# Two turns of activations by 32x32 blocks on VectorE, with feature rows numbered to match

## The chip, the cores and the metric

The kernel runs on one core of a Trainium2 chip. The metric is the device time of one execution in microseconds (us), the median of several runs. Every run gives one time; one further execution was recorded by the hardware profiler, and all rows quoted below come from that one.

## The reference, cut to what matters

One transformer block in float32 with S = 2048 tokens, D = 1024, 32 heads of 32, and an inner width of 3584:

```python
qkv = layernorm(x) @ wqkv                      # q, k, v by head
pq, pk = q @ w_phi, k @ w_phi                  # per head, 32x32
phi = concat(softmax(p), softmax(-p))          # for q and for k
o = phi_q (phi_k^T v) / (phi_q (phi_k^T 1) + 1e-6)
h = x + o @ wo
out = h + relu(layernorm(h) @ w1) @ w2
```

Both layer norms work on rows of tokens, and both products after them contract over the features. TensorE contracts over partitions, so x and h have to be turned: tokens on partitions before, features on partitions after.

## The kernel before

All large products run on TensorE with each float32 operand split in two float32r parts, a high and a low one, and three matmuls for each product (`mm3`, L180 to L183). A **step** is one `mm3`: three matmuls of 128x128 weights against 512 columns. The work of TensorE is a fixed list of **items**; an item has 8 steps before the MLP and 4 in it. Everything else is placed by hand: `when(step, f, ...)` puts the call of `f` behind the given step, and the engines then work their own rows in that order, each engine in order.

The items come in this sequence. Tokens are cut in 16 tiles of 128 (`t` = 0 to 15), in two halves of eight.

- Key and value items (`kv`) of the first half, four slabs of eight, then query items (`q`), two slabs of eight. Then the same for the second half. A slab uses the same 8 weight units for its eight tiles. Turned x stands in eight buffers `xT`, so that a tile of the second half is turned while the second query slab of the first half runs: tile `t` is normalised, turned by eight TensorE transposes (two bursts of four, `ln_turn`, L250), and copied out of PSUM as high part (ScalarE, L177) and low part (VectorE, L178).
- Attention's products (`at_num`, L678), spread over later items. Their inputs are turned by VectorE (`at_turn`, L664).
- 32 `wo` items, which give h. `wo_add` (L728) adds x on VectorE, `wo_store` (L731) writes h to DRAM. `ln_pair` then takes h back, two tiles at a time (one of each quarter of the tokens: the MLP's products are done by a scheme of seven products on sums of blocks, `UP` and `DOWN`), normalises them (L243), turns them by TensorE (L250 and L758, four bursts of four for a pair), copies them out of PSUM (L252, L759), forms the sums, and `ln_store` writes the seven operands `hs`. Four pairs belong to the first half (`b` = 0, during the `wo` items) and four to the second (`b` = 1, during the first half's up projection).
- Up projection and down projection of the MLP (`up_item`, `down_item`), first half, second half. `hT` is the turned h as the matmuls stream it.

Weights come through `Units`: SyncE's DMA queue loads a unit in one of 6 raw buffers, ScalarE copies the high part (L124), VectorE or GpSimd forms the low part (L128), into a ring of 10. In a slab 8 of the 10 are held, so the next slab's units 3 to 8 are split only as the last item of the old slab lets go of its units.

SyncE's queue (SP) issues nearly all DMAs, in order: weights, x, h, `hs` and the MLP's intermediate tensors. A DMA that waits for its data holds up all behind it.

Of the kernel before, what the change touches and what calls it, by code (L numbers as in the profile page):

```python
# [15 lines left out]
P = 128  # L16
# [123 lines left out]
def kernel(  # L140
# [68 lines left out]
    def ln_load(key, parts):  # L209
        xin[key] = xlp.tile([P, D], F32, name="xl") if key[0] == "x" and key[1] >= HT and key[1] % 4 > 1 else \  # L210
            lnp.tile([P, D], F32, name="xin")
        n = D // len(parts)
        for j, p in enumerate(parts):
            sp.dma_start(xin[key][:, j * n:(j + 1) * n], p)

    def ln_stats(key):
        src = xin[key]
        st = lnp.tile([P, 2, 6], F32, name="st", bufs=4)
# [21 lines left out]
    def ln_norm(key):  # L240
        sc, src = xst.pop(("s", key[1]) if key[0] == "x" and key[1] >= HT else key), xin.pop(key)
        xnt[key] = src if key[0] == "h" else fp_ln.tile([P, D], F32, name="xn")
        act.activation(xnt[key], src, AF.Identity, bias=sc[:, 1:2], scale=sc[:, 0:1])  # L243

    def ln_turn(key, j, dst=None):

        xn = xnt[key]
        pt = tp_bank().rearrange("p (k n) -> p k n", k=4)
        for k in range(4):
            pe.transpose(pt[:, k, :], xn[:, (4 * j + k) * P:(4 * j + k + 1) * P], ident)  # L250
        if dst is None:
            act.activation(xn[:, j * 512:(j + 1) * 512], pt.rearrange("p k n -> p (k n)"), AF.Copy)  # L252
            return
# [79 lines left out]
    def load(key, t):  # L333

        kind = key[0]
        if kind == "kv":
            _, hf, s, k = key
            sp.dma_start(t[:, 0:256], wpk[s][k])
            sp.dma_start(t[:, 256:512], wv[s, k])
        elif kind == "q":  # L340
            _, _, s, k = key
            sp.dma_start(t, wpq[s][k])
        elif kind == "wo":
            _, hf, c = key
            sp.dma_start(t, wo[hf, c])
        elif kind == "a":
            sp.dma_start(t, ad[key[1:]])
        else:
            _, _, m, p = key
            w = 1 if kind == "w1" else 2  # L350
            sp.dma_start(t, block(w, p, *{1: (0, 0), 2: (1, 0), 3: (1, 1)}[m]) if m < 4
                         else td[w, p][:, {5: 0, 7: 3 - w, 4: w, 6: 3}[m], :])

    def block(w, p, r, c):
# [359 lines left out]
    def wo_pair(tiles, hf, half, keys):  # L714
# [4 lines left out]
        for k in range(8):  # L719
# [5 lines left out]
            yield  # L725

    def wo_add(t, hf):
        v.tensor_add(xh[t, hf], wo_ps.pop((t, hf)), xh[t, hf])  # L728

    def wo_store(t, hf):  # L730
        sp.dma_start(hd[t][:, hf * 512:(hf + 1) * 512], xh.pop((t, hf)))  # L731

    def ln_pair(b, i, stage):

        keys = [("h", HT * b + 4 * r + i) for r in range(2)]
        if stage == 0:
            for key in keys:  # L740
                ln_load(key, [hd[key[1]]])
        elif stage == 1:
            for key in keys:
                ln_stats(key)
        elif stage == 2:
            for key in keys:
                ln_power(key)
        elif stage == 3:
            for key in keys:
                ln_norm(key)  # L750
        elif stage in (4, 5, 6):
            ln_turn(keys[stage // 6], stage != 4)
        elif stage == 7:
            x1, x2 = (xnt[key] for key in keys)
            s12 = (mp or hp).tile([P, 2, 512], F32, name="s12", bufs=1)
            pt = tp_bank()
            for k in range(4):
                pe.transpose(pt[:, k * P:(k + 1) * P], x2[:, k * P:(k + 1) * P], ident)  # L758
            act.activation(x2[:, 0:512], pt, AF.Copy)  # L759
            v.tensor_add(s12[:, 0, :], x2[:, 0:512], x2[:, 512:])  # L760
            v.tensor_sub(x2[:, 0:512], x1[:, 0:512], x2[:, 0:512])
            sums[b, i] = s12
        elif stage == 8:
            x1, s12 = xnt[keys[0]], sums[b, i]
# [12 lines left out]

    sums, hT = {}, {}

    def h_load(b, m, g):  # L780

        lo = hT[m][:, 1, :, 2 * g * P:2 * (g + 1) * P].rearrange("p k (i n) -> p k i n", i=2)
        for i in range(2):
            sp.dma_start(f32(lo[:, :, i, :]), hs[b, m][:, 2 * g + i, :].rearrange("p (k n) -> p k n", k=4))

    def h_parts(m, g):

        return (hT[m][:, s, :, 2 * g * P:2 * (g + 1) * P] for s in range(2))

# [167 lines left out]
    for t in range(1, NT):  # L957
# [4 lines left out]
        else:  # L962
# [12 lines left out]
        for j in range(2):  # L975
            when(stages[4 + j], ln_turn, ("x", t), j, lambda t=t: xT[t])
# [121 lines left out]
    LN2 = ((0, 9, 12, 17, 24, 25, 26, 27, 29, 36), (0, 18, 26, 32, 40, 42, 44, 46, 50, 60))  # L1100
# [219 lines left out]
```

## Time and profile before

| | |
|---|---|
| median of 3 runs | 1880.31 us (1879.95 to 1880.78) |
| the profiled execution's own time | 1881.49 us |
| its span, first to last instruction | 1879.7 us |
| granted TensorE clock | 1.000 |
| busy: TensorE matmul, weight load | 1872.6 us (100%), 1540.3 us |
| busy: VectorE, ScalarE, GpSimd | 1063.6, 741.0, 976.9 us |
| DMA | 433.21 MB, mean 230 GB/s |

PE is TensorE's matmuls, PEld its weight loads, DVE is VectorE, ACT ScalarE, POOL GpSimd, SPq the DMA queue of SyncE. A row of the timeline has the start in us, the time in us, the engine, the line, the operation, what it writes and reads, the shape and a count. Rows of grouped instructions end with busy time and the mean of one in ns, then idle time before them and what ended it. Matmuls overlap, and their ends are modelled: of PE, starts are to be read.

### The profile page before, as it was taken

The page shows a single profiled execution, that of the slowest core. Times are in us where ns is not written, and L with a number is a line of the kernel's source. Part 1 is how long each engine was busy: PE and PEld are TensorE (multiplying, and loading weights), DVE is VectorE, ACT ScalarE, POOL GpSimd, SP SyncE. Part 2 cuts the span into 40 slices and gives each one's busy share as a digit, 9 for nine tenths or more (in the row PEclk, how much of TensorE's full clock was granted, in tenths as well). Part 3 has the DMA queues.
Part 4 walks back from the last instruction along what each step waited for, and adds up shares of the span by engine and source line. Part 5 has one row for each costly group of instructions (what it writes and reads, how often), then busy time and mean ns, then how long its engine had stood idle before and what let it go on. Part 6 is the DMA issues. An engine that isn't in the chain of part 4 may idle for free.

```text
span 1879.7 us, 31869 instructions
## 1 busy us (share of the span) xinstructions
PE 1872.6 (100%) x11630; PEld 1540.3 (82%) x11630; DVE 1063.6 (57%) x1714; ACT 741.0 (39%) x1264; POOL 976.9 (52%) x956
## 2 busy tenths in 40 slices
PE   9999999999999999999999999999999999999999
PEld 7888888888888888888888888888888888888887
DVE  7788688677789777455444664444433333343333
ACT  5322244222233122355455554444444444444442
POOL 3778733677745988223343234445444444444443
PEclk9999999999999999999999999999999999999999
DMA  6889875454475567886877997877877677777775
GB/s 214 268 280 312 269 262 180 148 155 141 140 232 190 203 216 237 264 254 209 263 233 241 312 297 248 264 246 259 275 239 216 201 230 239 237 213 220 216 215 177
DMA packets 293036, 433.21 MB, mean 230 GB/s; under 512 B 24208, under 2 KB 150160, under 8 KB 292880
## 3 DMA queue, kind: packets, MB, share of 16 engines
q1 hardware_dynamic: 263712, 390.26, 65.3%
q10 hardware_dynamic: 29168, 40.93, 6.5%
q8 instruction: 91, 1.49, 0.3%
q14 instruction: 65, 0.53, 0.1%
HBM read 293.73 MB, written 137.36 MB: 229 GB/s over the span
## 4 chain that ended last, share of the span: by engine, by line
PE 98%; DVE 1%; ACT 0%; POOL 0%; DMA 0%; issue 0%; SPq 0%; DVEq 0%; POOLq 0%
PE mm L181 25%; PE mm L182 25%; PE mm L183 25%; PE ac L181 4%; PE ac L182 4%; PE ac L183 4%; PE tp L182 2%; PE tp L181 2%; PE tp L183 2%; PE tp L250 1%; PE tp L678 1%; PE ac L491 1%; PE ac L678 1%; PE tp L297 0%; DVE st L220 0%; PE tp L758 0%
## 5 line engine op out<-in xcount | busy, mean ns | idle before, releaser
L128 POOL TENSOR_TENSOR w<-raw,w 128x512 fp32r<-128x512 f32 x353 | 474.6, 1347 | 671.5 <-ACT w L124 638.0
L124 ACT ACTIVATE w<-raw 128x512 fp32r<-128x512 f32 x686 | 409.1, 626 | 491.8 <-PE mm L183 238.9
L128 DVE TENSOR_TENSOR w<-raw,w 128x512 fp32r<-128x512 f32 x333 | 275.0, 827 | 512.9 <-ACT w L124 507.3
L181 PE MATMUL mm<-w,xT 128*128 128x512 f32 x752 | 299.4, 398 | 0.0
L183 PE MATMUL mm<-w,xT 128*128 128x512 f32 x752 | 293.1, 390 | 0.0
L182 PE MATMUL mm<-w,xT 128*128 128x512 f32 x752 | 293.0, 390 | 0.0
L181 PE MATMUL mm<-hT,w 128*128 128x512 f32 x672 | 262.6, 391 | 0.0
L183 PE MATMUL mm<-hT,w 128*128 128x512 f32 x672 | 261.6, 389 | 0.0
L182 PE MATMUL mm<-hT,w 128*128 128x512 f32 x672 | 261.5, 389 | 0.0
L378 POOL TENSOR_TENSOR b<-b 128x256 f32<-128x256 f32 x168 | 129.0, 769 | 85.2 <-DMA b<-in_w_dram 75.4
L181 PEld LDWEIGHTS mm<-w,xT 128*128 128x128 f32 x752 | 141.2, 188 | 31.4 <-issue 2.2
L183 PEld LDWEIGHTS mm<-w,xT 128*128 128x128 f32 x752 | 141.2, 188 | 30.0
L182 PEld LDWEIGHTS mm<-w,xT 128*128 128x128 f32 x752 | 141.3, 188 | 28.5 <-issue 1.0
L181 PE MATMUL mm<-w 128*128 128x512 f32 x392 | 152.5, 389 | 0.0
L182 PE MATMUL mm<-w 128*128 128x512 f32 x392 | 152.5, 389 | 0.0
L183 PE MATMUL mm<-w 128*128 128x512 f32 x392 | 152.5, 389 | 0.0
L183 PEld LDWEIGHTS mm<-hT,w 128*128 128x128 f32 x672 | 126.1, 188 | 26.5
L181 PEld LDWEIGHTS mm<-hT,w 128*128 128x128 f32 x672 | 126.2, 188 | 25.8
L182 PEld LDWEIGHTS mm<-hT,w 128*128 128x128 f32 x672 | 126.2, 188 | 25.7
L480 POOL TENSOR_TENSOR zacc<-zacc,kphi 128x512 f32<-128x512 f32 x60 | 83.8, 1397 | 14.3 <-DVE kphi L472 14.3
L181 PEld LDWEIGHTS mm<-w 128*128 128x128 f32 x392 | 73.6, 188 | 15.3
L182 PEld LDWEIGHTS mm<-w 128*128 128x128 f32 x392 | 73.6, 188 | 15.3
(173 smaller groups left out, 3183.1 us busy)
## 6 DMA issues: line engine op xcount, KB each, us to landing
raw<-t SPq DMA_DIRECT2D x224, 256.0 KB, 4.0
raw<-ad SPq DMA_DIRECT2D x196, 256.0 KB, 3.0
raw<-in_w_dram SPq DMA_DIRECT2D x168, 256.0 KB, 3.2
ad<-c SPq DMA_DIRECT2D x112, 256.0 KB, 4.2
b<-in_w_dram SPq DMA_DIRECT2D x42, 512.0 KB, 5.7
t<-b SPq DMA_DIRECT2D x42, 512.0 KB, 3.6
ad<-s SPq DMA_DIRECT2D x84, 256.0 KB, 4.6
ed<-qe ACTq DMA_DIRECT2D x32, 512.0 KB, 3.9
```

Source lines behind the costliest of these rows:

```text
L124: nc.scalar.activation(w[:, 0, :], raw[1], AF.Copy)
L128: eng.tensor_tensor(out=w[:, 1, :], in0=raw[1], in1=w[:, 0, :].bitcast(F32), op=ALU.subtract)
L181: pe.matmul(ps, a_hi, b_hi, start=first, stop=False, skip_group_check=more)
L182: pe.matmul(ps, a_hi, b_lo, start=False, stop=False, skip_group_check=more)
L183: pe.matmul(ps, a_lo, b_hi, start=False, stop=last, skip_group_check=more)
L250: pe.transpose(pt[:, k, :], xn[:, (4 * j + k) * P:(4 * j + k + 1) * P], ident)
L378: pool.tensor_tensor(out=tsum[j, *out], in0=tsum[j, *a], in1=tsum[j, *b], op=ALU.subtract)
L480: pool.tensor_tensor(out=zacc[s], in0=zacc[s], in1=phi_of[key], op=ALU.add)
L491: pe.matmul(kv_ps[s][g][32 * i:32 * (i + 1), 0:64], vt[:, 32 * h:32 * (h + 1)], phi[:, 64 * h:64 * (h + 1)], start=first, stop=last)
L678: pe.matmul(banks[g][32 * c:32 * (c + 1), r * P:(r + 1) * P], kvL[rows, 4 * q + 2 * sd + h // 4, 32 * (h % 4):32 * (h % 4 + 1)], phT[rows, ...
```

## The change

The two turns that TensorE did, of x's second half and of h, are now done by VectorE's transposition of 32x32 blocks in place, over 128x1024 at once. Such an instruction turns each block but leaves the blocks where they are. What is missing, the exchange of blocks between groups of 32 partitions, is done by the load: a tile comes from DRAM in four DMAs, one for each group of 32 partitions.

- **x, second half.** `x_load` (4 DMAs for 1) puts 256 features of a group in each partition group. The norm's scale and bias, kept by token in `scx`, go through DRAM and back in that layout (`x_stats`, 5 small DMAs). `x_norm` is four ScalarE instructions of 256 elements, one for each group of tokens, in place of one of 1024, and picks its input with a step of 8 elements, so that feature `8p + k` ends on partition `p` in block `k`. `x_turn` is one VectorE instruction, `x_high` one ScalarE copy of 1024, `x_low_part` two GpSimd subtractions of 512. The second half's weight rows are read with the same numbering (`rows_of`): each partition's row lies 8 rows behind the one before.
- **h.** `wo_add` writes a new tile `xo` (features regrouped), `bn_stats` runs on it at once (`wo_stats`) and the scale is formed tile by tile (`wo_power`, `wo_keep`: a DMA of 8 bytes a partition). h lies in DRAM in pieces of 128 floats. `ln_pair` loads two tiles with 8 DMAs, the scales with 4, normalises with 8 ScalarE instructions of 256, and turns with 2 VectorE instructions; no transposes on TensorE, no copies out of PSUM.
- **hT** keeps the blocks as they come: the 512 columns that one matmul streams are now 16 runs of 32 floats, 128 floats apart (`h_chunk`), and no longer one run of 512.

```diff
-    hd = [dram.tile([P, D], F32, name=f"hd{t}") for t in range(NT)]
+    hd = [dram.tile([4, P, 2, P], F32, name=f"hd{t}") for t in range(NT)]
...
+    def x_load(t):
+        xin["x", t] = (xlp if t % 4 > 1 else lnp).tile([P, D], F32, name="xl" if t % 4 > 1 else "xin")
+        src = x[t * P:(t + 1) * P, :].rearrange("(g j) (a f) -> a j g f", g=4, a=4)
+        for a in range(4):
+            sp.dma_start(xin["x", t][32 * a:32 * (a + 1)].rearrange("p (g f) -> p g f", g=4), src[a])
...
+    def turn_norm(dst, src, scale, bias):
+        for g in range(4):
+            c = slice(256 * g, 256 * (g + 1))
+            out, in_ = (dst[:, c], src[:, c]) if len(src.shape) == 2 else \
+                (dst[:, c].rearrange("p (k i) -> p k i", i=32), src[:, g])
+            act.activation(out, in_, AF.Identity, bias=bias(g), scale=scale(g))
+    def x_norm(t):
+        src = xin.pop(("x", t))
+        xnt["x", t] = xn = fp_ln.tile([P, D], F32, name="xn")
+        turn_norm(xn, src.rearrange("p (g i k) -> p g k i", g=4, k=NK), ...
+    def x_turn(t):
+        v.transpose(xn, xn)
+    def x_high(t):
+        act.activation(hi, xn, AF.Copy)
+    def x_low_part(t, j):
+        pool.tensor_tensor(out=lo[:, k], in0=xn[:, k], in1=f32(hi[:, k]), op=ALU.subtract)
...
-            sp.dma_start(t[:, 0:256], wpk[s][k])
+            sp.dma_start(t[:, 0:256], rows_of(wpk[s], hf, k))
...
+        return w[k] if hf == 0 else w.rearrange("c (p k) f -> k (c p) f", k=NK)[k]
...
     def wo_add(t, hf):
-        v.tensor_add(xh[t, hf], wo_ps.pop((t, hf)), xh[t, hf])
+        v.tensor_add(by_row(xo[t, hf]), by_group(wo_ps.pop((t, hf))), by_group(xh.pop((t, hf))))
+    def wo_stats(t, hf):
+        v.bn_stats(out=st[:, 6 * hf:6 * hf + 6], in_=xo[t, hf])
...
-        elif stage in (4, 5, 6):
-            ln_turn(keys[stage // 6], stage != 4)
...
+        elif stage in (2, 3):
+            turn_norm(hx[tiles[r]], hx[tiles[r]], ...
+        elif stage in (4, 5):
+            ht = hx[tiles[stage - 4]]
+            v.transpose(ht, ht)
...
     def h_load(b, m, g):
-        for i in range(2):
-            sp.dma_start(f32(lo[:, :, i, :]), hs[b, m][:, 2 * g + i, :].rearrange("p (k n) -> p k n", k=4))
+        sp.dma_start(f32(h_parts(m, g)[1]), hs[b, m][:, 2 * g:2 * g + 2, :])
+    def h_chunk(m, s, k):
+        return hT[m][:, s].rearrange("p i (g k j) -> p k (i g) j", g=4, k=4)[:, k]
...
-            mm3(ps, w[:, 0, cols], w[:, 1, cols], hT[m][:, 0, k, :], hT[m][:, 1, k, :],
+            mm3(by_token(ps), w[:, 0, cols], w[:, 1, cols], h_chunk(m, 0, k), h_chunk(m, 1, k),
...
-            stages = (load_, None, None, turn - 8, turn, turn + 3)
+            for step, f, *args in ((-4, x_norm), (0, x_turn), (3, x_high), (5, x_low_part, 0), (7, x_low_part, 1)):
+                when(turn + step, f, t, *args)
...
-    LN2 = ((0, 9, 12, 17, 24, 25, 26, 27, 29, 36), (0, 18, 26, 32, 40, 42, 44, 46, 50, 60))
+    LN2 = ((0, 5, 17, 20, 23, 25, 26, 27, 32), (0, 18, 32, 36, 40, 44, 48, 50, 60))
```

`LN2` holds, in steps after a pair's start, the place of each stage of `ln_pair`.

Two places show what moves. The first is ScalarE where the second query slab of the first half ends and the second half's first slab of keys begins. `w<-raw` are the copies of the new weight units, `qe<-qe` is the exponential of a query item, `xn` the norm of x, `xT` the turned x. Before:

```order
L177 ACTIVATE xT<-tp 128x512
L567 ACTIVATE qe<-qe 128x1024
L569 DMA ed_80<-qe 128x4x256
L124 ACTIVATE w<-raw 128x512
L177 ACTIVATE xT<-tp 128x512
L243 ACTIVATE xn<-xl,scx 128x1024
L124 ACTIVATE w<-raw 128x512 x3
L177 ACTIVATE xT<-tp 128x512
L124 ACTIVATE w<-raw 128x512 x2
L567 ACTIVATE qe<-qe 128x1024
```

And now, the same stretch:

```order
L257 ACTIVATE xT<-xn 128x1024
L239 ACTIVATE xn<-xl,srx 128x256 x4
L618 ACTIVATE qe<-qe 128x1024
L620 DMA ed_80<-qe 128x4x256
L124 ACTIVATE w<-raw 128x512 x4
L257 ACTIVATE xT<-xn 128x1024
L124 ACTIVATE w<-raw 128x512
L239 ACTIVATE xn<-xl,srx 128x256 x4
L124 ACTIVATE w<-raw 128x512
L618 ACTIVATE qe<-qe 128x1024
```

Two copies out of PSUM became one copy of 1024 that follows VectorE's turn. That copy stands ahead of the fifth of the six weight copies and the fourfold norm ahead of the sixth; before, the norm stood behind the first and a copy out of PSUM behind the fourth.

The second is VectorE around the first pair of h tiles during the `wo` items. `oT`, `qtz`, `qden` and `qe` are attention's, L664 (now L715) is the turn that `at_num` waits for, L728 (now L793) is `wo_add`. Before:

```order
L664 STREAM_TRANSPOSE qe<-qe 128x1024 x2
L626 TENSOR_REDUCE qtz<-ez 128x16 x2
L728 TENSOR_TENSOR xh<-mm,xh 128x512
L626 TENSOR_REDUCE qtz<-ez 128x16 x2
L760 TENSOR_TENSOR s_7882<-xin 128x512
L761 TENSOR_TENSOR xin<-xin 128x512
L643 RECIPROCAL qden<-qden 128x16
L695 TENSOR_TENSOR oT<-tp,oT 128x8x32 x2
L695 TENSOR_TENSOR oT<-ac,oT 128x8x32 x2
```

And now:

```order
L715 STREAM_TRANSPOSE qe<-qe 128x1024 x2
L838 STREAM_TRANSPOSE xin<-xin 128x1024
L677 TENSOR_REDUCE qtz<-ez 128x16 x2
L793 TENSOR_TENSOR xo<-mm,xh 128x4x4x32
L838 STREAM_TRANSPOSE xin<-xin 128x1024
L677 TENSOR_REDUCE qtz<-ez 128x16 x2
L797 BN_STATS qmx<-xo 128x6
L842 TENSOR_TENSOR s_7884<-xin 128x512
L843 TENSOR_TENSOR xin<-xin 128x4x128
L694 RECIPROCAL qden<-qden 128x16
```

The pair's two turns (L838) stand between attention's, and the statistics come behind each `wo_add` and no longer in one block.

More of the change, by code (lines that the diff above doesn't have):

```diff
@@ L196 @@
     ed = [dram.tile([P, 8, 4, 256], F32, name=f"ed{b}") for b in range(4)]
-    hd = [dram.tile([P, D], F32, name=f"hd{t}") for t in range(NT)]
+    hd = [dram.tile([4, P, 2, P], F32, name=f"hd{t}") for t in range(NT)]
+    sxd = dram.tile([P, 2 * HT], F32, name="sxd")
+    shd = {(b, i): dram.tile([P, 2, 2], F32, name=f"shd{b}_{i}") for b in range(2) for i in range(4)}
     hs = {(b, m): dram.tile([P, 4, 512], F32, name=f"hs{b}_{m}") for b in range(2) for m in UP}
@@ L209, in ln_load @@
     def ln_load(key, parts):
-        xin[key] = xlp.tile([P, D], F32, name="xl") if key[0] == "x" and key[1] >= HT and key[1] % 4 > 1 else \
-            lnp.tile([P, D], F32, name="xin")
+        xin[key] = lnp.tile([P, D], F32, name="xin")
         n = D // len(parts)
@@ L214, in ln_load, with x_stats, x_parts @@
             sp.dma_start(xin[key][:, j * n:(j + 1) * n], p)
+    def x_load(t):
[3 more added lines that the diff above has]
+            sp.dma_start(xin["x", t][32 * a:32 * (a + 1)].rearrange("p (g f) -> p g f", g=4), src[a])
+    def x_stats(step):
+        if step == 0:
+            sp.dma_start(sxd, scx.rearrange("p t c -> p (t c)"))
+            return
+        src = sxd.rearrange("(g j) c -> j g c", g=4)
+        for a in range(4):
+            sp.dma_start(srx[32 * a:32 * (a + 1)], src)
+    def turn_norm(dst, src, scale, bias):
[7 more added lines that the diff above has]
+        xnt["x", t] = xn = fp_ln.tile([P, D], F32, name="xn")
+        turn_norm(xn, src.rearrange("p (g i k) -> p g k i", g=4, k=NK), lambda g: srx[:, g, 2 * (t - HT):2 * (t - HT) + 1],
+                  lambda g: srx[:, g, 2 * (t - HT) + 1:2 * (t - HT) + 2])
+    def x_turn(t):
+        xn = xnt["x", t]
+        v.transpose(xn, xn)
+    def x_parts(t):
+        return [xT[t][:, s].rearrange("p k (g j) -> p k g j", g=4) for s in range(2)], \
+            xnt["x", t].rearrange("p (g k j) -> p k g j", g=4, k=NK)
+    def x_high(t):
+        (hi, _), xn = x_parts(t)
+        act.activation(hi, xn, AF.Copy)
+    def x_low_part(t, j):
+        (hi, lo), xn = x_parts(t)
+        k = slice(4 * j, 4 * j + 4)
+        pool.tensor_tensor(out=lo[:, k], in0=xn[:, k], in1=f32(hi[:, k]), op=ALU.subtract)
+        if j == 1:
+            del xnt["x", t]
     def ln_stats(key):
         src = xin[key]
-        st = lnp.tile([P, 2, 6], F32, name="st", bufs=4)
+        st = lnp.tile([P, 16], F32, name="st", bufs=4)[:, 0:12].rearrange("p (j c) -> p j c", j=2)
         for j in range(2):
@@ L240, in ln_norm, with ln_turn @@
     def ln_norm(key):
-        sc, src = xst.pop(("s", key[1]) if key[0] == "x" and key[1] >= HT else key), xin.pop(key)
-        xnt[key] = src if key[0] == "h" else fp_ln.tile([P, D], F32, name="xn")
+        sc, src = xst.pop(key), xin.pop(key)
+        xnt[key] = fp_ln.tile([P, D], F32, name="xn")
         act.activation(xnt[key], src, AF.Identity, bias=sc[:, 1:2], scale=sc[:, 0:1])
-    def ln_turn(key, j, dst=None):
+    def ln_turn(key, j, dst):
         xn = xnt[key]
@@ L736, in ln_pair, with wo_keep @@
+    def wo_keep(t):
+        sp.dma_start(shd[t // HT, t % 4][:, t % HT // 4, :], hst.pop(t)[:, 14:16])
+    hst, hst_pair, xo = {}, {}, {}
     def ln_pair(b, i, stage):
-        keys = [("h", HT * b + 4 * r + i) for r in range(2)]
+        tiles = [HT * b + 4 * r + i for r in range(2)]
         if stage == 0:
-            for key in keys:
-                ln_load(key, [hd[key[1]]])
-        elif stage == 1:
[L743 to L750, printed above, removed]
-        elif stage in (4, 5, 6):
-            ln_turn(keys[stage // 6], stage != 4)
-        elif stage == 7:
[L754 to L764, printed above, removed]
@@ new lines, in ln_pair @@
+            for t in tiles:
+                hx[t] = lnp.tile([P, D], F32, name="xin")
+                src = hd[t].rearrange("a (g j) r c -> a j g (r c)", g=4)
+                for a in range(4):
+                    sp.dma_start(hx[t][32 * a:32 * (a + 1)].rearrange("p (g c) -> p g c", g=4), src[a])
+        elif stage == 1:
+            hsr[b, i] = sr = lnp.tile([P, 16], F32, name="st", bufs=4)
+            src = shd[b, i].rearrange("(g j) r c -> j g (r c)", g=4)
+            for a in range(4):
+                sp.dma_start(sr[32 * a:32 * (a + 1)].rearrange("p (g c) -> p g c", g=4), src)
+        elif stage in (2, 3):
+            r, sr = stage - 2, hsr[b, i]
+            turn_norm(hx[tiles[r]], hx[tiles[r]], lambda g: sr[:, 4 * g + 2 * r:4 * g + 2 * r + 1],
+                      lambda g: sr[:, 4 * g + 2 * r + 1:4 * g + 2 * r + 2])
+        elif stage in (4, 5):
+            ht = hx[tiles[stage - 4]]
+            v.transpose(ht, ht)
+        elif stage == 6:
+            x1, x2 = (hx[t] for t in tiles)
+            s12 = (mp or hp).tile([P, 2, 512], F32, name="s12", bufs=1)
+            v.tensor_add(by_half(s12[:, 0, :]), h_half(x2, 0), h_half(x2, 1))
+            v.tensor_sub(h_half(x2, 0), h_half(x1, 0), h_half(x2, 0))
+            sums[b, i] = s12
+        elif stage == 7:
+            x1, s12 = hx[tiles[0]], sums[b, i]
@@ L786, in h_parts @@
     def h_parts(m, g):
-        return (hT[m][:, s, :, 2 * g * P:2 * (g + 1) * P] for s in range(2))
+        return [hT[m][:, s, 2 * g:2 * g + 2, :] for s in range(2)]
     def h_high(m, g):
@@ L796, in h_low, with by_token @@
         v.tensor_sub(lo, f32(lo), f32(hi))
+    def by_token(ps):
+        return ps.rearrange("p (t j) -> p t j", j=32)
+    def h_chunk(m, s, k):
+        return hT[m][:, s].rearrange("p i (g k j) -> p k (i g) j", g=4, k=4)[:, k]
     bank = {}
@@ L974 @@
         do(n, 0, x_open, t)
-        for j in range(2):
+        for j in range(2 if t < HT else 0):
             when(stages[4 + j], ln_turn, ("x", t), j, lambda t=t: xT[t])
@@ L1168 @@
     W = Units(nc, wraw, wring, load, ready, steps)
-    half = consts.tile([P, 1], F32, name="half")
+    small = consts.tile([P, 8], F32, name="small")
+    half, eps = small[:, 0:1], small[:, 1:2]
     pool.memset(half, -0.5)
-    eps = consts.tile([P, 1], F32, name="eps")
     pool.memset(eps, DEN_EPS / 2)
-    act.activation(consts.tile([P, 1], F32, name="first"), half, AF.Exp)
+    act.activation(small[:, 2:3], half, AF.Exp)
     scx = consts.tile([P, HT, 2], F32, name="scx")
-    consts.tile([P, 56], F32, name="fill")
+    srx = consts.tile([P, 4, 2 * HT], F32, name="srx")
+    consts.tile([P, 8], F32, name="fill")
     ln_load(("x", 0), [x[0:P, 0:512], x[0:P, 512:1024]])
```

93 lines of the change are left out of this document (67 added, 26 removed).

## The prediction

> **What bounds the kernel now.** I read the page first: busy times, the clock, the chain that ended last.
>
> ```profile
> PE 1872.6 (100%) x11630; PEld 1540.3 (82%) x11630; DVE 1063.6 (57%) x1714; ACT 741.0 (39%) x1264; POOL 976.9 (52%) x956
> ...
> PEclk9999999999999999999999999999999999999999
> ...
> PE 98%; DVE 1%; ACT 0%; POOL 0%; DMA 0%; issue 0%; SPq 0%; DVEq 0%; POOLq 0%
> ```
>
> TensorE is busy all the time, at full clock in every slice, and the chain of work is TensorE's to 98%. Second, who TensorE waited for, in full:
>
> ```profile
> PE tp L1193 <- POOL ones L1189: 1.6, 1, 1.6
> PE tp L1212 <- ACT xn L237: 1.2, 1, 1.2
> PE tp L250 <- ACT xn L243: 0.4, 1, 0.4
> PE mm L541 <- DVE w L415: 0.2, 1, 0.2
> ```
>
> That is 3.4 us, and the first two belong to the start. So the span is the sum of what TensorE issues. What is taken off its list comes off the time, as long as its inputs still come in time.
>
> Third, what a burst of transposes costs. Durations don't tell: matmuls overlap. Starts do (timeline of TensorE; start, time, line, and so on):
>
> ```profile
> 663.73 0.39 PE L182 MATMUL mm<-w,oT 128*128 128x512 f32 x1
> ...
> 666.67 0.40 PE L183 MATMUL mm<-w,oT 128*128 128x512 f32 x1
> 666.91 0.60 PE L250 MATMUL tp<-ident,xin 128*128 128x128 f32 x4
> 667.27 0.47 PE L181 MATMUL mm<-w,oT 128*128 128x512 f32 x1
> 667.58 0.39 PE L182 MATMUL mm<-w,oT 128*128 128x512 f32 x1
> ...
> 313.99 0.39 PE L183 MATMUL mm<-w,xT 128*128 128x512 f32 x1
> 314.22 0.60 PE L250 MATMUL tp<-ident,xn 128*128 128x128 f32 x4
> 314.57 0.48 PE L181 MATMUL mm<-w,xT 128*128 128x512 f32 x1
> 314.89 0.40 PE L182 MATMUL mm<-w,xT 128*128 128x512 f32 x1
> ```
>
> From 663.73 to 666.67 lie 13 starts: 2.94 / 13 = 0.226 us for a matmul. From 666.67 two matmuls and a burst of four transposes take 0.91 us, without the burst 0.452: a burst costs 0.458 us. At x (313.99 to 314.89) it is 0.90 - 0.452 = 0.448. I take 0.45.
>
> **The change, part by part.** The bursts, from the groups by line, engine and shape:
>
> ```profile
> L250 PE MATMUL tp<-ident,xn 128*128 128x128 f32 x120 | 18.1, 273 | 0.5 <-ACT xn L243 0.4
> L250 PE MATMUL tp<-ident,xin 128*128 128x128 f32 x96 | 14.4, 272 | 0.0
> L758 PE MATMUL tp<-ident,xin 128*128 128x128 f32 x32 | 4.8, 272 | 0.0
> L518 PE MATMUL tp<-zacc,ones 128*128 128x512 f32 x8 | 4.1, 591 | 0.0
> L297 PE MATMUL tp<-wt,wphi 32*32 32x256 f32 x224 | 10.2, 385 | 0.0
> ```
>
> The 120 of x are 15 tiles of 8; the 7 of the first half stay, 64 go. Of h all 96 + 32 go. 192 transposes are 48 bursts: 48 x 0.45 = 21.6 us less on TensorE (ends 21.5 and 22.0 by the two readings).
>
> *The streamed operand.* The up projection's 784 x 3 = 2352 matmuls now read 16 runs of 32 floats. No row has this for such matmuls. The nearest: L297 streams 256 columns in eight runs of 32. Between 272 ns (L250, 128 columns in one run) and 591 ns (L518, 512 in one run) a straight line gives 378 at 256, and L297 took 385: 7 ns for seven breaks, 1 ns for a break, if it is that at all (its array tile is smaller, and ends are modelled). So the bounds are 0 and 15 x 1 x 2352 = 35 us; a gain is excluded, since the 512 columns are the same. I take 0, as the row fits one line with the unbroken ones within 2%. The Trainium skill, Advanced Engine Details and Errata, section Memory Cachelines, has lines of 16 bytes in SBUF, and full speed as long as at least two accesses in a row fall on one line; runs of 128 bytes keep that, so its sum is the same; no run here shows it for this operand.
>
> *The work that goes to other engines.* Prices:
>
> ```profile
> L664 DVE STREAM_TRANSPOSE qe<-qe 128x1024 f32<-128x1024 f32 x28 | 34.2, 1227 | 12.1 <-POOL qe L658 9.5 <-POOL qe L648 1.7 <-DMA xh<-in_x_dram 1.0
> L178 DVE TENSOR_TENSOR xT<-tp,xT 128x512 fp32r<-128x512 f32 x30 | 20.3, 678 | 6.1 <-ACT xT L177 6.1
> L243 ACT ACTIVATE xn<-xl,scx 128x1024 f32<-128x1024 f32 x4 | 4.9, 1234 | 0.0
> L237 ACT ACTIVATE xn<-xin,sc 128x512 f32<-128x512 f32 x2 | 1.6, 816 | 2.7 <-POOL sc L231 2.7
> L792 ACT ACTIVATE hT<-hT 128x1024 fp32r<-128x1024 f32 x28 | 29.6, 1056 | 30.5 <-DMA hT<-hs 29.5 <-DMA raw<-in_w_dram 1.1
> L177 ACT ACTIVATE xT<-tp 128x512 fp32r<-128x512 f32 x30 | 17.9, 597 | 33.2 <-PE tp L250 33.1
> L252 ACT ACTIVATE xin<-tp 128x512 f32<-128x512 f32 x24 | 14.4, 599 | 24.2 <-PE tp L250 22.8 <-DVE qden L643 1.3
> L128 POOL TENSOR_TENSOR w<-raw,w 128x512 fp32r<-128x512 f32 x353 | 474.6, 1347 | 671.5 <-ACT w L124 638.0 <-DMA raw<-t 8.9 <-DVE c L822 5.6
> ```
>
> A norm of 256: from 816 at 512 and 1234 at 1024, 0.82 ns an element and 0.40 us fixed, so 0.61 us, and four of them 2.4 where one took 1.2. The ends for x, which reads with a step of 8: not below 1.2 for the four; with the price of an element doubled, 4 x (0.40 + 0.42) = 3.3. I take 2.4, as these are the rows of the same operation. Here the same section speaks against the change: a step of 32 bytes meets a new line with each element, which it calls a penalty without a figure; doubled, as an estimate, it is the upper end.
>
> Per tile of x: ScalarE 2.4 + 1.06 for 1.2 + 2 x 0.6, so +1.0 (8 in all); VectorE 1.23 for 2 x 0.68, so -0.1; GpSimd 2 x 1.35 = +2.7 (22 in all). Per tile of h: ScalarE 2.4 for 1.2 + 2 x 0.6, even; VectorE +1.23 (20 in all), the sums and `wo_add` as before; `bn_stats` and the power are moved from a pair's start to each `wo` item. None of this is on TensorE's chain while it is early enough. Is it? Two stretches are the tightest:
>
> ```profile
> 264.00:316.00 52.00, 52.00 (x261) 42.97 (x260) 45.28 (x69) 30.00 (x40) 14.91 (x16) 1.00 0.69 226
> 640.00:700.00 60.00, 60.00 (x843) 48.59 (x844) 42.14 (x74) 12.12 (x24) 51.56 (x66) 1.00 0.66 222
> ...
> 307.56 1.66 ACT L124 ACTIVATE w<-raw 128x512 fp32r<-128x512 f32 x3
> 309.60 1.14 ACT L124 ACTIVATE w<-raw 128x512 fp32r<-128x512 f32 x2
> 311.48 1.19 DVE L128 TENSOR_TENSOR w<-raw,w 128x512 fp32r<-128x512 f32 x1
> 316.28 0.39 PE L182 MATMUL mm<-w,xT 128*128 128x512 f32 x1
> 630.94 0.25 DVE L643 RECIPROCAL qden<-qden 128x16 f32<-128x16 f32 x1 [1.51 <-POOL qden L640]
> 631.11 1.19 DVE L664 STREAM_TRANSPOSE qe<-qe 128x1024 f32<-128x1024 f32 x1
> 633.00 0.28 PE L678 MATMUL ac<-qe,kvL 32*32 32x128 f32 x2
> ```
>
> (Stretches: length, then busy time and count of PE, PEld, DVE, ACT, POOL.) In the first, where x is turned, VectorE works 45.3 of 52 us. The stretch loses 16 bursts, 7.2 us, and VectorE only 1: 44.3 of 44.8, no slack left there. Each item lasts 24 x 0.226 = 5.4 us; its new loop (turn 1.23, high copy 1.06, next norm 2.4, next turn) takes 4.7, with the dear norm 5.6. At its end six weight copies follow; the last unit's low part was ready at 311.48 + 1.19 = 312.67 and is first read at 316.28, 3.6 us of cover. TensorE now comes 0.9 earlier (two bursts less in that item), and ScalarE is about 1 us later, so some 1.7 remain: a loss of 0 to 2 us there. In the second stretch attention's turn ended at 632.30 and the unit's second half is read by 633.00: 0.7 us of cover, with two `bn_stats` now put ahead, some 1.3 us, against 1.5 us in which VectorE waited for GpSimd just before: 0 to 0.6 us. I take 0.8 us lost in all.
>
> *DMA and SP.* x: 8 x 3 more and 5 for the scales; h: 16 x 3 more, 16 + 32 small ones; `h_load` 28 less: +97 DMAs.
>
> ```profile
> L214 SPq DMA_DIRECT2D xin<-hd x16: 319/320/1097, 644.2 to 994.8; - x16
> ...
> SPq L351 <- POOL w L128: 259.2, 231, 9.6
> ```
>
> At 0.32 to 1.1 us each SP issues 31 to 107 us more. It waited 259 us for raw buffers alone in the MLP, so there it has time. The strided weight rows are as many pieces of the same size: nothing. The sharpest moment is a pair's 8 loads, 2.6 to 8.8 us of SP, with x for the next `wo_add` behind them. h is needed 17 steps (11.5 us) after the first issue.
>
> **The sum.** The profiled execution took 1881.5 us: span 1879.7 and 1.8 around it. 1879.7 - 21.6 + 0.8 = 1858.9, and 1860.7 with what lies around. The median of the runs lies 1.2 below that execution: 1859.5 us.
>
> **The rivals.** What a measurement can tell from no change is about 0.2%, 3.8 us.
>
> - *The queues give back a part.* ScalarE's loop at x slips past 5.4 us, or h's loads hold up SP so that `wo_add` waits in VectorE's queue and attention's turns behind it come late. For it: covers of 0.7 to 3.6 us, VectorE without slack at x. Against it: only eight tiles and four pairs. At 0.2 us a tile and 1 to 2 us a pair it is 2 to 9 us: 1861 to 1868.
> - *Slower: the broken stream costs time.* TensorE itself is the place, in the up projection. The price is 1 ns a break, 15 ns a matmul, 35 us: 1859 + 35 = 1894. It decides from 21.6 us / 2352 = 9 ns a matmul on. For it: the 7 ns of L297. Against it: the tile and the modelled ends.
> - *The two nearly cancel*, a stream cost of 7 to 10 ns: no change.
> - *Durations are the cost:* 192 x 0.272 = 52 us, 1829. The starts above exclude it nearly.
>
> **How the numbers follow.** Forecast 0.70, with its own range 1858 to 1861; queues 0.20; slower 0.06; cancel 0.03; durations 0.01. The range 1858 to 1867 holds the first and nearly all of the second. Faster by over 0.2%: 0.70 + 0.20 + 0.01 = 0.91; within 0.03; slower 0.06.
>
> **What would show it.** Right: no transposes of h on TensorE, the PE instruction count down by 192; spacing in the up projection still 0.226 us; TensorE's waits below 5 us in all. Wrong: a spacing above 0.23 there; waits of TensorE for `w` near 309 us or for attention's turn near 626 us (the times above less 7.2); ScalarE waiting for h's loads.

## The result, and the profile after

The changed kernel takes 1910.23 us (median of 6 runs, 1904.74 to 1913.36) against 1880.55 us for the kernel before on the same chip: a ratio of 1.0152, 95% interval 1.0135 to 1.0169. It is 1.5% slower, where 1.1% faster was forecast. The profiled execution took 1904.74 us, its span 1903.0 us. It is the fastest of the six: the median lies 5.5 us above it, and of the other five there is no trace, so the account below holds for this execution alone. From the page of the changed kernel, busy time and the chain that ended last:

```profile
PE 1882.3 (99%) x11438; PEld 1523.5 (80%) x11438; DVE 1076.5 (57%) x1722; ACT 750.3 (39%) x1296; POOL 997.9 (52%) x972
...
PE 76%; POOL 9%; DMA 5%; DVE 5%; issue 3%; ACT 2%; SPq 0%; ACTq 0%; POOLq 0%; DVEq 0%
```

TensorE issues 11630 - 11438 = 192 instructions less, the 48 bursts. Yet its busy time is up by 9.7 us, and the chain is TensorE's to 76% only: GpSimd, DMA and VectorE stand in it. Two things came in.

**The up projection's matmuls are slower.** One of their groups of instructions before (count, then busy time in us and the mean of one in ns):

```profile
L181 PE MATMUL mm<-hT,w 128*128 128x512 f32 x672 | 262.6, 391 | 0.0
```

The same group in the changed kernel:

```profile
L181 PE MATMUL mm<-hT,w 128*128 128x512 f32 x672 | 269.0, 400 | 0.0
```

And of the changed kernel's timeline (start, time) the first and the last of 26 successive starts:

```profile
999.82 0.40 PE L182 MATMUL mm<-hT,w 128*128 128x512 f32 x1
...
1005.74 0.40 PE L183 MATMUL mm<-hT,w 128*128 128x512 f32 x1
```

5.92 us / 25 = 0.237 us from start to start, where 0.227 was before. All other matmuls kept 0.227. 10 ns x 2352 = 23.5 us.

**TensorE waits.** Who waited for whom on TensorE after (total, times, longest; the waits of the start, which were there before, left out):

```profile
PE mm L182 <- POOL w L128: 4.5, 4, 1.6
PE tp L729 <- issue: 3.2, 3, 2.5
PE tp L729 <- DVE qe L715: 2.2, 3, 1.1
PE mm L182 <- DVE hT L884: 1.8, 1, 1.8
...
PE mm L181 <- ACT w L124: 0.9, 1, 0.9
```

And three of the stretches in which they lie (us from A to B, length, busy time of PE, PEld, DVE, ACT, POOL with counts, granted clock, DMA share, GB/s):

```profile
303.00:313.00 10.00, 7.89 (x24) 4.97 (x24) 7.06 (x9) 8.63 (x13) 8.26 (x7) 0.83 0.66 183
...
754.00:768.00 14.00, 11.35 (x157) 8.86 (x158) 6.92 (x12) 1.21 (x4) 5.48 (x12) 0.76 0.74 208
824.00:840.00 16.00, 14.19 (x54) 10.91 (x53) 12.40 (x13) 10.41 (x16) 3.92 (x2) 0.89 0.76 262
```

The waits cost more than themselves, as the granted clock falls behind them: it lost 0.17 x 10 + 0.24 x 14 + 0.11 x 16 = 6.8 us of work. Set side by side, start by start, the gaps between the same matmuls grew by 4.1 us at 303 to 313 us, 5.2 at 354 to 453, 9.7 at 700 to 764 and 3.7 at 828 to 836, half clock included: 22.7 us. The account: -48 x 0.447 (bursts) + 23.5 (stream) + 22.7 (waits) = +24.7; from 12 us on TensorE's work runs 1.4 us ahead of the trace of before, which leaves the +23.3 us by which the spans differ. The medians differ by 29.7 us; the 6.4 us between the two are not accounted for.

What made the waits, place by place. At the change from q to kv (ScalarE) TensorE waits for the first of the new weight units, 0.93 and 0.86 us:

```profile
299.34 3.17 ACT L239 ACTIVATE xn<-xl,srx 128x256 f32<-128x256 f32 x4
302.43 1.04 ACT L618 ACTIVATE qe<-qe 128x1024 f32<-128x1024 f32 x1
303.91 2.19 ACT L124 ACTIVATE w<-raw 128x512 fp32r<-128x512 f32 x4 [0.44 <-ACT qe L618]
...
304.59 0.49 PE L181 MATMUL mm<-w,xT 128*128 128x512 f32 x1 [0.93 <-ACT w L124]
305.95 0.50 PE L182 MATMUL mm<-w,xT 128*128 128x512 f32 x1 [0.86 <-POOL w L128]
```

The first copy stands behind the norm of tile 14, four times 0.8 us, and an exponential. It starts at 303.91 us, 1.0 us earlier than before (304.87), but TensorE had come at 303.5, where it first read these weights at 312.06 before: 15 of the 16 bursts of x lie ahead of this place. The norm of tile 15 between the fifth and the sixth copy (307.47, below) comes after these two waits; a last wait of 0.24 us at 311.9 follows it. In the kv stage (SP and GpSimd) the sums of MLP weights run as one serial loop: the store of a set waits for its sums, the load of the next (`b`) stands behind the store, and GpSimd stands still for it, with the next slab's `w` behind:

```profile
307.47 3.13 ACT L239 ACTIVATE xn<-xl,srx 128x256 f32<-128x256 f32 x4
...
341.14 0.53 SPq L432 DMA_DIRECT2D t<-b  x1
341.76 0.57 SPq L419 DMA_DIRECT2D b<-in_w_dram  x1
...
346.70 3.52 POOL L429 TENSOR_TENSOR b<-b 128x256 f32<-128x256 f32 x4 [4.32 <-DMA b<-in_w_dram]
...
354.85 1.71 POOL L128 TENSOR_TENSOR w<-raw,w 128x512 fp32r<-128x512 f32 x1
```

From load to load it took 10.0 and 10.8 us there, and 9.3 and 10.3 before: hardly longer, but TensorE came 4.2, 2.3 and 0.4 us earlier than before to the three places (at 354, 404 and 453 us), and GpSimd to the sums it waited for only 0.4 us earlier, then 0.9 and 2.4 us later. In the attention stage GpSimd works off LN2's sums (L848, L850) ahead of attention's scales (L709), then VectorE turns (L715), then TensorE starts, up to 2.5 us late. The sums stood ahead of a scale before, too (742.37 to 745.29 us); new ahead of them is the power of the statistics (L809 to L811), for which GpSimd now waits for VectorE:

```profile
746.88 0.55 POOL L809 TENSOR_SCALAR qmx<-qmx 128x1 f32<-128x1 f32 x1 [1.30 <-DVE qmx L799]
...
748.82 1.29 POOL L848 TENSOR_TENSOR s<-s,xin 128x512 f32<-128x512 f32 x1
750.19 1.29 POOL L850 TENSOR_TENSOR s4l<-xin,s 128x512 f32<-128x512 f32 x1
...
752.27 1.91 POOL L709 TENSOR_TENSOR qe<-qe,qsd 128x1024 f32<-128x1024 f32 x1
...
754.47 1.91 POOL L709 TENSOR_TENSOR qe<-qe,qsd 128x1024 f32<-128x1024 f32 x1
...
756.41 1.25 DVE L715 STREAM_TRANSPOSE qe<-qe 128x1024 f32<-128x1024 f32 x1 [0.95 <-POOL qe L709]
...
757.71 0.47 PE L729 MATMUL tp<-qe,kvL 32*32 32x128 f32 x8 [1.09 <-DVE qe L715]
```

At 828 us, in the up projection, TensorE waits for the seventh operand (hT7) though it comes 4.5 us later than before: the first load of hT7 was issued 8.4 us later (first row) than before (second row), behind weight loads for which SP had to wait:

```profile
817.96 0.38 SPq L872 DMA_DIRECT2D hT<-hs  x1
```

```profile
809.55 0.93 SPq L784 DMA_DIRECT2D hT<-hs  x2
```

### The profile page after: what moved, and what is told of

Read it like the earlier page. It is cut to its first block, busy times and chain, and to the rows that moved or that the text cites. A ratio compares the mean times of both kernels' runs of the same rounds, so it can differ in the third digit from the quotient of the medians.

```text
span 1903.0 us, 31666 instructions
## 1 busy us (share of the span) xinstructions
PE 1882.3 (99%) x11438; PEld 1523.5 (80%) x11438; DVE 1076.5 (57%) x1722; ACT 750.3 (39%) x1296; POOL 997.9 (52%) x972
## 4 chain that ended last, share of the span: by engine, by line
PE 76%; POOL 9%; DMA 5%; DVE 5%; issue 3%; ACT 2%; SPq 0%; ACTq 0%; POOLq 0%; DVEq 0%
PE mm L181 19%; PE mm L183 19%; PE mm L182 19%; PE ac L183 4%; PE ac L181 4%; PE ac L182 4%; PE tp L182 2%; PE tp L181 2%; PE tp L183 2%; DMA b<-in_w_dram 2%; POOL ez L670 2%; POOL b L429 2%; POOL qe L709 1%; POOL zacc L531 1%; POOL w L128 1%
## 5 line engine op out<-in xcount | busy, mean ns | idle before, releaser
L182 PE MATMUL mm<-hT,w 128*128 128x512 f32 x672 | 268.4, 399 | 1.8 <-DVE hT L884 1.8
L183 PE MATMUL mm<-hT,w 128*128 128x512 f32 x672 | 269.3, 401 | 0.0
L181 PE MATMUL mm<-hT,w 128*128 128x512 f32 x672 | 269.0, 400 | 0.0
L515 ACT ACTIVATE ke<-ke 128x512 f32<-128x512 f32 x64 | 40.4, 631 | 134.5 <-DVE ke L511 134.5
L181 PEld LDWEIGHTS mm<-w 128*128 128x128 f32 x392 | 73.6, 188 | 15.3
```

The lines of the kernel that those rows point to most:

```text
L181: pe.matmul(ps, a_hi, b_hi, start=first, stop=False, skip_group_check=more)
L182: pe.matmul(ps, a_hi, b_lo, start=False, stop=False, skip_group_check=more)
L183: pe.matmul(ps, a_lo, b_hi, start=False, stop=last, skip_group_check=more)
L515: act.activation(e_of[key], e_of[key], AF.Exp)
```

## The experiments

Each has the kernel before beside it on the same chip (1880.8 to 1881.4 us).

**1. What a broken stream costs, by length of run.** The kernel before, another run length for each of the seven products:

```diff
+RUN = {1: 512, 5: 128, 6: 64, 2: 32, 7: 16, 3: 8, 4: 1}
...
+    def h_runs(m, s, k):
...
+        return hT[m][:, s].rearrange("p a b -> p (a b)").rearrange("p (t k j) -> p k t j", k=4, j=RUN[m])[:, k]
...
-            mm3(ps, w[:, 0, cols], w[:, 1, cols], hT[m][:, 0, k, :], hT[m][:, 1, k, :],
+            mm3(in_runs(ps, m), w[:, 0, cols], w[:, 1, cols], h_runs(m, 0, k), h_runs(m, 1, k),
```

> The kernel before, with one thing changed: in the up projection each of the seven products streams its 512 columns of hT in another number of runs (product 1: 1 run of 512 floats, 5: 4 of 128, 6: 8 of 64, 2: 16 of 32, 7: 32 of 16, 3: 64 of 8, 4: 512 of 1, 16 bytes apart). The chunks of h are mixed up by it, so only times are read. 336 matmuls for each product. Theory A, a price for each break: 10 ns for 15 breaks is 0.67 ns for one, so the spacings are 227, 229, 232, 237, 248, 269 ns and some 570 ns for single floats, in all 336 x 0.42 us = 141 us more, about 2020 us. Theory B, a price for short runs as such: 227 ns down to runs of 64, about 237 ns for 32 and for all shorter ones, some 1893 us. Rival: the stride costs nothing and after's 237 ns come from something else in its second half: 227 ns for all seven, 1880 us.

Measured: 1973.26 us, in one execution. One of the three matmuls of each product, from the groups of TensorE (`h_one` is 1 run of 512, `h_four` 4 of 128, `h_eight` 8 of 64, `h_sixteen` 16 of 32, `h_thirty` 32 of 16, `h_sixty` 64 of 8, `h_all` 512 of 1):

```profile
L185 PE MATMUL mm<-h_all,w 128*128 128x512 f32 x112 | 72.0, 643 | 0.0
...
L185 PE MATMUL mm<-h_thirty,w 128*128 128x512 f32 x112 | 45.6, 407 | 0.0
...
L185 PE MATMUL ac<-h_sixteen,w 128*128 128x512 f32 x112 | 44.8, 400 | 0.0
...
L185 PE MATMUL mm<-h_sixty,w 128*128 128x512 f32 x112 | 44.2, 395 | 0.0
...
L185 PE MATMUL mm<-h_one,w 128*128 128x512 f32 x112 | 43.8, 391 | 0.0
...
L185 PE MATMUL mm<-h_four,w 128*128 128x512 f32 x112 | 43.6, 389 | 0.0
L185 PE MATMUL mm<-h_eight,w 128*128 128x512 f32 x112 | 43.6, 389 | 0.0
```

Start to start, from runs of 512 down to single floats, it is 227, 227, 227, 237, 243, 235 and 461 ns (the median of each product); 336 x (10 + 16 + 8 + 234) = 90 us, and 92 were measured. Both theories are wrong: 4 or 8 runs cost nothing, so it is no price for each break; and from 16 runs on the price goes up, down and far up, so it is no single step either. What stands: runs of 64 floats, placed as here, are free, runs of 32 are not.

**2. The stream alone, in the kernel before.** All products with `RUN` = 32, nothing else of the change.

> The kernel before, with all 2352 matmuls of the up projection streaming hT in 16 runs of 32 floats, as the changed kernel does, and nothing else of the change (the chunks of h are mixed up, so only times are read). If the stream is the cause: 237 ns for each, 2352 x 10 ns = 23.5 us, 1904 us, with no new wait on TensorE. If the 10 ns come from the way hT is written or loaded in the changed kernel: 227 ns and 1880 us.

Measured: 1903.56 us, ratio 1.0119 (1.0106 to 1.0132), 237 ns start to start, TensorE's waits 4.0 us, all but 0.6 of them at the start. 22.7 us more than before by the stream alone, as expected. The half of the loss that lies in the up projection is settled.

**3. The stream made whole, in the changed kernel.** VectorE's turn can put its blocks elsewhere. Four turns of 128x512, each into a part that is free by then, bring the chunks of h in a row:

```diff
-            v.transpose(ht, ht)
+            moves = ((by_half(s12[:, 0, :]), h_half(x1, 0)), (h_half(x1, 0), h_half(x1, 1))) if stage == 4 else \
+                ((h_half(x1, 1), h_half(x2, 0)), (h_half(x2, 0), h_half(x2, 1)))
+            for to, of in moves:
+                v.transpose(to.rearrange("p k (g j) -> p g k j", g=4), of.rearrange("p g (k j) -> p g k j", k=4))
...
-        return hT[m][:, s].rearrange("p i (g k j) -> p k (i g) j", g=4, k=4)[:, k]
+        return hT[m][:, s, k, :].rearrange("p (t j) -> p t j", j=32)
```

> The changed kernel, with the order of h's columns made right while VectorE turns them (the turn writes feature chunk, group, token in place of group, feature chunk, token, through the free halves of the two tiles), so that each chunk of hT lies in 512 floats in a row; hT comes in two loads of 256 KB again. Stream theory: spacing 227 ns, 23.5 us less, stalls as in the changed kernel: 1881 us against its profiled 1904.7 us, 1881 to 1887 with the spread of its runs. Rival, something else holds the up projection at 237 ns: 1905 to 1911 us. Rival, the splits of w1 can't follow 12 matmuls in 2.72 us: TensorE waits for w, 1885 to 1900 us.

Measured: 1891.62 us, ratio 1.0054 (1.0041 to 1.0067); the spacing is 227 ns again. Of the 23.5 us 18.6 came by the medians, 15.7 by the profiled executions, as the waits grew from 22.7 to 30.0 us. TensorE waits for h itself now; this version needs a second load for each part of hT, but that this is the reason is not shown by this run:

```profile
PE mm L181 <- ACT hT L887: 3.4, 1, 3.4
...
PE mm L182 <- DVE hT L891: 2.7, 1, 2.7
```

**4. The waits alone, in the changed kernel.** The stream stays broken; four places are moved:

```diff
+            if t >= NT - 2:
+                turn = 398 if t == NT - 2 else 410
...
-        when(step + (13 if not far and step < up0 else 17), t_store, w, p, j)
+        when(step + (16 if not far and step < up0 else 17), t_store, w, p, j)
...
-            pool.tensor_tensor(out=by_half(s12[:, 1, :]), ...
+            eng = pool if b else v
+            eng.tensor_tensor(out=by_half(s12[:, 1, :]), ...
...
-            step = up0 + (... else 6 * (j - 4) + 10 + 2 * g)
+            step = up0 + (... else 6 * (j - 4) + 4 + 2 * g)
```

> The changed kernel with its strided stream left as it is and four moves against its stalls: x tiles 14 and 15 are normed, turned and split 21 and 25 steps later, behind the change from q to kv; the store of each weight sum in the kv stages stands three steps later, behind the next set's load; s12[1] and s4 of the first four pairs of LN2 are made by VectorE instead of GpSimd; hT7 to hT4 of the first half load six steps earlier. Theory, the stalls are queues that the removed transposes no longer cover: 304 to 312 us (4.9), 354 to 453 us (4.6), 705 to 764 us (10) and 828 us (3.6) all go, 1904.7 - 20 = 1885 us or a little more. Rival, in the attention stage VectorE is as full as GpSimd: its 10 us stay, 1893 to 1898 us. Rival, what is freed at 304 us makes the kv stage wait for the weight sums instead: 1890 us and waits on GpSimd's w at 350 to 460 us.

Measured: 1891.17 us (1889.24 to 1899.46), ratio 1.0059 (1.0045 to 1.0074): 19.1 us less than the changed kernel by the medians, 13.1 by the profiled executions. By place, in the trace: 354 to 453 us 5.2 to 0, 828 us 3.7 to 0, 303 to 313 us 4.1 to 3.1 (with a wait at 337 us), attention 9.7 to 5.3, and 0.6 came new at 586 us; 9.0 us remain. So at the two places that went to 0 it was queues in the wrong order and not a lack of engine time; at the first place and in attention this run leaves it open.

**5. The x part alone, in the kernel before.** `x_load` to `x_low_part`, `x_stats` and `rows_of`; nothing of h.

> The kernel before, with the change's x part alone: x tiles 8 to 15 loaded by partition group, turned by VectorE, split by ScalarE and GpSimd, and the second half's weight rows 8p+k; h stays on TensorE and its stream whole. Theory, the part's gain is eaten where it is made: 16 bursts of 0.447 us go (-7.2), stalls at 304 to 312 us (+4.9) and at 354 to 453 us (+4.6) come, 1880.9 + 2.3 = 1883 us. Rival, those stalls belong to the h part: 1880.9 - 7.2 = 1873.7 us.

Measured: 1883.81 us over 11 runs (1880.84 to 1888.69), ratio 1.0015 (1.0006 to 1.0023): its gain is eaten where it is made, as expected. TensorE's waits in it:

```profile
PE mm L182 <- POOL w L128: 3.3, 4, 1.2
...
PE mm L181 <- ACT w L124: 1.4, 2, 1.2
PE mm L182 <- DVE w L128: 1.1, 2, 0.9
```

Side by side with the trace of before the gaps grew by 8.7 us at 303 to 312 and 354 to 455 us, against 16 x 0.447 = 7.2 us of bursts; 1.5 us were gained at the start here too, and the spans are equal (1879.7 us). The granted clock stayed at 1.0.

**6. Run, distance or start?** As the first run, with other placings; each entry has the run, the distance from run to run and the start, in floats:

```diff
+RUN = {1: (32, 64, 0), 5: (64, 128, 32), 6: (512, 512, 32), 2: (32, 96, 0), 7: (16, 32, 0), 3: (8, 16, 0), 4: (1, 2, 0)}
```

> The kernel before, with another placing of the stream for each product of the up projection (336 matmuls each; the chunks of h are mixed up, so only times are read): product 1: runs of 32 floats, 64 apart; 2: runs of 32, 96 apart; 5: runs of 64, 128 apart, from float 32; 6: 512 in a row from float 32; 7: runs of 16, 32 apart; 3: runs of 8, 16 apart; 4: single floats, 2 apart. Theory, what counts is the length of a run, with nothing to pay from 64 floats on: 237 ns for products 1 and 2, 227 for 5 and 6, 243 for 7, 235 for 3. Rival, what counts is the distance: 1, 2, 7, 3 differ from the 237, 237, 243, 235 ns that runs of 32, 16 and 8 took at four times their length, and singles 2 apart are nearer 227 than the 461 ns at 4 apart. Rival, the start counts: 5 and 6 above 230 ns.

Measured: 1970.37 us, in one execution. `h_pair` is 32 of every 64, `h_thirds` 32 of every 96, `h_whole_shifted` 512 in a row from float 32, `h_single` every second float:

```profile
L184 PE MATMUL mm<-h_single,w 128*128 128x512 f32 x112 | 70.8, 632 | 0.0
...
L185 PE MATMUL mm<-h_pair,w 128*128 128x512 f32 x112 | 44.8, 400 | 0.0
...
L185 PE MATMUL mm<-h_whole_shifted,w 128*128 128x512 f32 x112 | 44.2, 394 | 0.0
L185 PE MATMUL ac<-h_thirds,w 128*128 128x512 f32 x112 | 43.8, 391 | 0.0
```

Start to start, as means: pair 237, thirds 229 (median 227), runs of 64 from float 32 232, whole from float 32 232, 16 of 32 240, 8 of 16 233, singles 452 ns. The length doesn't decide alone (pair and thirds, both of runs of 32, differ by 8 ns), nor does the distance (singles cost nearly as much at 2 as at 4), and the start counts: 512 floats in a row cost 5 ns more from float 32. No theory here fits all fourteen, and that stays open. The kernel needs only what both runs agree on: from a start at a multiple of 64 floats, a whole row costs nothing, nor do runs of 64 and 128 as placed in the first run.

**7. Both, and two places more.** Runs 3 and 4 together, the norm of x behind the exponentials, and LN2's turns and sums between attention's turns.

> The changed kernel with the stream made whole as in the third run and the moves of the fourth, and two more: in the q stage the norm of x stands behind the exponentials (turn, high and low parts 3 steps later with it), and in the first LN2 the turns and sums of each pair stand between the attention's turns. Theory, the stream and the stalls add: the fourth run's profiled 1891 us less 23.5 is 1868, less what it still stalls (2.2 us at 305, 5 us at 700 to 714) 1860 to 1863 us, faster than both kernels. Rival, with the stream whole the waits move on as they did in the third run (28.7 us of stalls there, 21.4 in the changed kernel): 1866 to 1876 us.

Measured: 1877.78 us over 11 runs (1874.84 to 1881.98), ratio 0.9983 (0.9974 to 0.9992): faster than before, by less than I count as a difference. The rival had the direction right and was still too low: 19.8 us of waits remain, 10.7 of them in the attention stage. Two rows of VectorE's timeline show one maker: LN2's operations, which I had put just ahead of attention's turns (L715), hold these up, and a subtraction of 0.7 us took 1.67 us there. The third row shows another: `wo_add` waits.

```profile
676.04 1.67 DVE L849 TENSOR_TENSOR xin<-s,xin 128x512 f32<-128x512 f32 x1
...
678.95 2.36 DVE L715 STREAM_TRANSPOSE qe<-qe 128x1024 f32<-128x1024 f32 x2
...
736.18 0.69 DVE L793 TENSOR_TENSOR xo<-mm,xh 128x512 f32<-128x512 f32 x1 [6.47 <-issue]
```

The wait is put down to "issue", but the timeline of SP's queue shows its operand `xh` issued 6.1 us before, behind eight loads of h that took 5 us to issue; the loads of `xh` around it landed up to 6.0 us after their issue:

```profile
723.15 4.98 SPq L826 DMA_DIRECT2D xin<-hd  x8
...
730.09 0.36 SPq L753 DMA_DIRECT2D xh<-in_x_dram  x1
```

**8. The remaining queues put in order.** The seventh run's kernel with the moves that the expectation lists, all at once:

```diff
-        xh[t, hf] = hp.tile([P, 512], F32, name="xh", bufs=2)
+        xh[t, hf] = hp.tile([P, 512], F32, name="xh", bufs=3)
-        xo[t, hf] = hp.tile([P, 512], F32, name="xo", bufs=3)
+        xo[t, hf] = hp.tile([P, 512], F32, name="xo", bufs=2)
...
-        when(8 * n - 4 if n > wo_first + 1 else wo0, wo_load, t, hf)
+        when(8 * n - 12 if n > wo_first + 1 else wo0, wo_load, t, hf)
...
+    FIRST_LN2 = ((0, 5, 17, 20, 40, 41, 42, 43, 44), (8, 13, 24, 26, 32, 33, 34, 35, 36),
+                 (0, 5, 17, 19, 24, 25, 26, 27, 28), (0, 5, 17, 20, 23, 25, 26, 27, 32))
...
+            if t >= NT - 3:
+                turn = 395 + 12 * (t - NT + 3)
```

> The seventh run's kernel (stream whole, moves against the stalls) with its remaining waits taken in turn: x's wo tiles get 3 buffers and load 12 steps ahead in place of 4 (xo 2 buffers), since VectorE's add waited 6.47 us for one at 736 us; each LN2 pair's eight loads stand in two groups six steps apart; the first three pairs' turns and sums stand behind the attention's turns they held up at 679 us; hs is laid out so that hT is one load of 1 KB pieces; x tile 13 also goes behind the change to kv, and the low parts of tiles 13 to 15 to VectorE. Theory, each place is a queue and nothing else: 19.3 us of stalls fall to 5 or less, 1862 to 1866 us. Rival, VectorE and GpSimd are full in the attention stage and no order helps: 7 to 12 us stay there, 1868 to 1874 us. Rival, the added work on VectorE at 310 to 350 us delays kv: new waits there, 1870 us or more.

Measured: 1865.45 us (1862.29 to 1868.98), ratio 0.9919 (0.9906 to 0.9933): faster than the kernel before by 0.8% and than the changed one by 2.3%. TensorE's waits, complete but for two below 0.5 us:

```profile
PE tp L729 <- issue: 1.8, 1, 1.8
PE tp L1337 <- ACT xn L287: 1.6, 1, 1.6
PE tp L1318 <- POOL ones L1314: 1.6, 1, 1.6
PE tp L729 <- DVE qe L715: 0.7, 1, 0.7
```

The profiled execution took 1862.29 us, its span 1860.5 us, with 3.9 us of gaps left, at 303 to 307 and at 740 us. What each of the moves gave is not shown.

## Why the prediction was wrong, by its own steps

- *The bursts* were right: 192 instructions less, 48 x 0.447 = 21.5 us. With the two losses repaired (run 8) the span is 1860.5 us in the profiled execution, the forecast one 1858.9; the median, 1865.45, is 6.0 us above the forecast 1859.5.
- *The streamed operand* is the step that failed. The one row for it, L297, lay 7 ns above the straight line, 1 ns a break; that gave 35 us as the upper end, and I took 0 "as the row fits one line with the unbroken ones within 2%". It cost 10 ns for 15 breaks, 23.5 us. Two per cent of a matmul is 4.5 ns, half of the 9 ns from which I had written that the change turns slower: a tolerance that the decision couldn't bear. The right mechanism stood there as a rival with a chance of 0.06; a bound of 15 ns that reached past the break-even of 9 deserved far more. Its price for each break was wrong too (run 1: 3 or 7 breaks cost nothing). I was also led by the Trainium skill, Advanced Engine Details and Errata, section Memory Cachelines, by whose lines of 16 bytes, as I read them, runs of 128 bytes keep full speed; the trace disagrees (237 against 227 ns), and the measurement decides.
- *The stalls*, 0.8 us, are the second failed step: 22.7 us, more than what the bursts gave. Their mechanism was the rival "the queues give back a part", sized at 2 to 9 us. The change to kv was named, with 0 to 2 us; it cost 4.1. I let TensorE come 0.9 us earlier there, by the two bursts of the last item, and looked at the last of the six weight units; TensorE came 8.5 us earlier (303.5 against 312.06), by 15 bursts and its earlier start, and waited for the first unit. The attention turn was named, with 0 to 0.6; the stage cost 9.7, as I looked at one of its turns and not at GpSimd, which worked 51.6 of the 60 us that I had quoted and lost none of its work when TensorE lost its bursts; run 4 took 4.4 of the 9.7 back, two sums moved from GpSimd to VectorE among its moves. The kv stage (5.2) and hT7 (3.7) were not looked at: to the kv stage TensorE came earlier, and at hT7 the load came 8.4 us later than before, TensorE 4.5.
- *The half clock* behind a wait, 6.8 of the 22.7 us, was not in the sum at all.
- *The norms*: for h four took 4 x 0.59 = 2.4 us, as worked out; for x, with a step of 8, 4 x 0.87 = 3.5 us, above the upper end of 3.3. Here the same section of the Trainium skill, which I had weighed and set aside, was right (each element on a line of its own is dear), and this put 1.1 us a tile on ScalarE, ahead of the weight copies from 303.9 us on:

```profile
L239 ACT ACTIVATE xin<-xin,st 128x256 f32<-128x256 f32 x64 | 32.8, 589 | 29.6 <-DMA st<-shd 12.0 <-DMA hd<-xo 11.0 <-DVE qden L694 6.6
L239 ACT ACTIVATE xn<-xin,srx 128x256 f32<-128x256 f32 x16 | 12.8, 874 | 0.4 <-DMA raw<-in_wv_dram 0.4
```

- *DMA and SP* had no term in the sum. In the changed kernel SP's order stands behind the waits of the kv stage and of hT7. The pair's eight loads with `xh` behind them, named as "the sharpest moment", show in run 7: VectorE waited 6.5 us for `xh`, and TensorE 3.5 us at 735 us after it. That the `xh` buffers went from 5 to 2 stood in the change and was in no term.

## What to carry to other kernels

A cut on the engine that bounds a kernel is worth what the second engine of each stage has in hand there: for every stage from the change on, also the unchanged ones, set its cover (when an input is ready, when it is read) against how much earlier the bound engine will come. A layout that is made free on one side is paid where it is streamed: two thousand matmuls turn 10 ns into the whole gain, so a broken stream is measured first, or mended where an instruction writes anyway. And when a rival's break-even is 9 ns, a fit within 2% of 227 ns is no ground to set it to zero.

## What the runs showed of the hardware that was not expected

- A 128x512 matmul's streamed operand: 227 ns for 1 run of 512, 4 of 128 or 8 of 64 floats; 237 for 16 of 32, 243 for 32 of 16, 235 for 64 of 8, 461 for single floats 16 bytes apart; 232 for a whole row that starts at float 32 (runs 1 and 6). The order isn't explained.
- The granted clock was 0.5 for about 3.4, 6.7 and 3.5 us (two times the lost share in the stretches shown: 0.17 x 10, 0.24 x 14, 0.11 x 16) behind waits as short as 0.93 and 0.86 us, which ended 1.4 us apart. In run 5 waits of 1.2 and 0.9 us at the same place left it at 1.0, so the length of the waits alone does not decide. The Trainium skill, TensorE: Matmul & The Clock Gate, Part 1, has windows of 3413 ns, which agrees; its table has the clock low after an idle window of about 3.4 us, and in the changed kernel the longest wait shortly before a fall was 2.5 us, which does not agree.
- VectorE's turn of 128x512 into another order of blocks took 709 ns (run 3), two of them 1.42 us, where one of 128x1024 in place took 1.23 us: 0.2 us more for the same data, with one instruction more.
